# First batch of a fused attention and feed-forward kernel: loads issued at once into places of their own, products of zeros before the first data, weight roundings one step earlier, attention steps one at a time

## The chip, the cores and the metric

One core of a Trainium2 chip. The time is the device time of one execution in microseconds (us), median over several executions. The kernel before takes 1046.3 us (median of 3; in the runs beside the changed kernel 1046.53). The granted clock is the share of its full clock that TensorE was given, 1.00 or 0.50 in these records; the mean of a stretch can lie between.

## The reference, cut to what matters

```python
def _attn_ref(q, k, v, g_norm):              # 8 batches, 8 heads, 576 rows, 64 columns, float32
    kv = np.einsum('bhsd,bhse->bhde', k, v)  # no softmax: k and v meet first
    out = np.einsum('bhsd,bhde->bhse', q, kv)
    rms = np.sqrt(np.mean(out * out, axis=-1, keepdims=True) + 1e-06)
    return out / rms * g_norm

def _moe_ref(x, w_in, w_out):                # x: 4608 x 512; w_in 512 x 2048; w_out 2048 x 512
    h = x @ w_in
    g = np.maximum(0.01 * h, h)
    return g @ w_out
```

The attention's output, with the heads side by side, is x. The tokens go through the two large products in nine blocks of 512. One batch is 576 rows, so block 0 holds most of batch 0, and the remaining 64 rows of batch 0 (the tail) and the first 448 rows of batch 1 make up block 1; both are computed beside block 0's products.

## The kernel before: what the change and the argument touch

From block 1 on, the products use a scheme with seven products for eight (h_a, h_b, h_c, o_a and so on). Block 0 is computed with plain products, because the weights are still arriving and being rounded. It alternates four products of 512 columns into `h_ps` (one for each row group e of one weight job) with four into `o_acc` (one for each 128 tokens), 16 times. Each counts as two instructions in the profile, so such a group is a row of `x8`; the very first `h_ps` comes in two halves of 256 columns, together a row of `x16`. After each pair, `between(n)` emits weight roundings and attention steps.

The names in the profile: `kv_ps` is k times v of one pair of heads, `q_ps` and `rest_ps` are the turned q, `o_ps` is one quarter of the attention's output, `sq` its square, `ss_ps` the sums of squares. `h_ps` is the first large product, `gT` its activation (on ScalarE), `o_acc` the second large product, `h_a` the first product of block 1. A rounding is two pieces on ScalarE (`add`, `cut`) and four on VectorE, the second of them the shift.

```python
    def load_pair(b, p):                       # two heads: k, v, q; ring of two buffers per name
        hs = slice(2 * p, 2 * p + 2)
        k_ins[b, p] = load_rows(nc.sync, k[b, hs], "k")
        v_ins[b, p] = load_rows(nc.sync, v[b, hs], "v")
        if b == 0:
            q_ins[b, p] = load_rows(nc.scalar, q[b, hs], "q")
            return
        ...
    load_pair(0, 0)
    load_pair(0, 1)
    ...
    w1_sb = [[consts.tile([P, NE, U * P], F32, name=f"w1_{h}_{c}") for c in range(NC)]
             for h in range(2)]               # one tile holds U = 2 jobs: job u writes [:, :, u*P:(u+1)*P]
    ...
        # the rounding of one job, 128 x 512 numbers:
        pin(nc.scalar.activation(add, lo, func=AF.Copy, scale=2.0 ** -29))                  # L153 / L173
        pin(nc.scalar.activation(cut, hi.bitcast(F32), func=AF.Copy, scale=2.0 ** -112))    # L155 / L175
        pin(nc.vector.tensor_scalar(cut, cut, HIGH_MOST, -HIGH_MOST, ...))                  # L156 / L176
        pin(nc.vector.tensor_scalar(dst, cut, 3, None, op0=ALU.logical_shift_left))         # L159 / L179
        pin(nc.vector.scalar_tensor_tensor(dst, in0=cut, scalar=0x80000000, in1=dst, ...))  # L160 / L180
        pin(nc.vector.tensor_tensor(dst, dst, add, op=ALU.add))                             # L162 / L182
    ...
    def outputs(b, lo, hi, e, sums, o_ps):     # one quarter of the attention's output
        ...
        sq = work.tile([P, n], F32, tag="t2k", name="sq", bufs=4)   # four places, shared with add and cut
        nc.scalar.activation(sq, o_ps, func=AF.Square)
        nc.scalar.activation(x[:, e, :], o_ps, func=AF.Copy, scale=g_sb[:, e:e + 1])
        if sums is None:
            return sq
        nc.vector.tensor_add(sums, sums, sq)
        return sums
    ...
    def first_attention():                     # batch 0, half blocks of 256 columns
        for p in range(NP):
            attention_kv(0, p, kv_ps)          # 10 small products, x20 in the profile
            ...                                # 8 + 2 products with the identity turn q (x16, x4)
            if p < 2:
                load_pair(0, p + 2)            # pairs 2 and 3 reuse the buffers of 0 and 1
        ...
    loaded, rounded = 7, 3
    def between(n):
        nonlocal a_steps, loaded, rounded
        while rounded < min(2 + (18 * n + 6) // 7, 2 * n + 5, len(w_jobs)):
            ...
            round_w(rounded)
            rounded += 1
        if n == 3:
            go(a_steps)                        # the tail in one piece
            a_steps = attention(1)
        if n > 6:
            go(a_steps, 2 if n > 8 else 1)     # batch 1's steps in groups
```

## Time and profile before

| | before |
|---|---|
| median, range | 1046.53 us, 1046.02 to 1046.81 (4 runs beside the changed kernel) |
| TensorE busy | 1000.2 us, 96% |
| first quarter of the output (`o_ps`) starts | 27.43 us |
| first full row of `h_ps` starts, after its wait | 46.56 us |
| block 0 over, first `h_a` starts | 183.52 us |
| from there to the end of the span | 861.2 us |

The last four rows come from starts of rows in TensorE's timeline. Two of the lines behind the table are these, the others are in the prediction:

```profile
27.43 4.50 PE L85 MATMUL o_ps<-qT,kv 128*32 128x256 f32 x40 [0.81 <-DVE qT L309]
...
183.52 1.89 PE L85 MATMUL h_a<-xT,w 128*128 128x256 f32 x8
```

### The profile page before, as it was taken

Reading aid. Unit: us, or ns where it says so; the run is one execution under the profiler, and the core shown is the slowest. Engines: PE = TensorE matmul, PEld = TensorE weight load, DVE = VectorE, ACT = ScalarE, POOL = GpSimd, SP = SyncE. Lnnn points to the kernel's source line nnn. Section 1 sums busy time; section 2 is a strip of 40 time slices with the busy share of each in tenths; the row PEclk is TensorE's granted clock in tenths of the full one; section 3 lists DMA queues with packets and bytes.
Section 4 is the critical chain, followed back from the end, with each engine's and each line's share of the span. In section 5 each row is a group of like instructions: output and inputs, shape, how many; then the busy total and the mean of one; then the engine's idle time right before and its main releaser. Section 6 shows DMA issues by size and latency. Waiting matters only on the chain.

```text
span 1044.7 us, 13017 instructions
## 1 busy us (share of the span) xinstructions
PE 1000.2 (96%) x5146; PEld 777.3 (74%) x5146; DVE 426.5 (41%) x591; ACT 264.5 (25%) x497; POOL 505.1 (48%) x403
## 2 busy tenths in 40 slices
PE   5589989999999999999999999999999999999997
PEld 4334434778888778888888788877887788888886
DVE  1557678224531463235323543344314521332123
ACT  1444343232213221322122311321132212111210
POOL 2000021456655665555555555555555656666641
PEclk9799999999999999999999999999999999999999
DMA  8356750710052004300340024000300010001001
GB/s 214 124 151 201 212 150 0 193 29 1 1 154 67 1 1 109 112 1 1 94 127 1 1 80 142 1 1 19 113 1 1 1 41 1 1 0 41 1 0 41
DMA packets 45309, 63.41 MB, mean 61 GB/s; under 512 B 5312, under 2 KB 39104, under 8 KB 45248
## 3 DMA queue, kind: packets, MB, share of 16 engines
q1 hardware_dynamic: 34560, 51.95, 18.2%
q10 hardware_dynamic: 10432, 10.62, 3.2%
q8 instruction: 41, 0.67, 0.3%
q14 instruction: 20, 0.16, 0.1%
q0 software_dynamic: 256, 0.00, 0.0%
HBM read 53.12 MB, written 9.44 MB: 60 GB/s over the span
## 4 chain that ended last, share of the span: by engine, by line
PE 89%; DVE 6%; DMA 2%; issue 1%; ACT 1%; SPq 1%; POOL 0%; ACTq 0%; DVEq 0%
PE o_a L85 21%; PE h_a L85 21%; PE h_c L85 10%; PE o_c L85 10%; PE h_ps L85 5%; PE o_b L85 5%; PE h_b L85 5%; PE o_ps L85 3%; PE o_acc L85 3%; PE kv_ps L85 2%; DVE rms L253 1%; PE ss_ps L85 1%; DMA v_in<-in_v_dram 1%; DVE w L160 1%; DMA q_in<-in_q_dram 1%
## 5 line engine op out<-in xcount | busy, mean ns | idle before, releaser
L85 PE MATMUL o_a<-wt,gs 128*128 128x256 f32 x512 | 124.8, 386 | 2.9 <-DVE o L330 1.9
L330 DVE TENSOR_TENSOR o<-o_a,o 128x512 f32<-128x512 f32 x104 | 71.4, 687 | 129.9 <-PE o_a L85 129.9
L85 PEld LDWEIGHTS o_a<-wt,gs 128*128 128x128 f32 x512 | 94.1, 190 | 28.5 <-issue 10.8
L330 POOL TENSOR_TENSOR wt<-w,w 128x512 f32<-128x512 f32 x32 | 40.9, 1277 | 153.4 <-PE o_a L85 150.1
L330 POOL TENSOR_TENSOR ws<-w 128x512 f32<-128x512 f32 x32 | 44.3, 1386 | 135.1 <-PE h_a L85 98.8
L330 POOL TENSOR_TENSOR ws<-w,w 128x512 f32<-128x512 f32 x32 | 42.5, 1328 | 131.5 <-DMA raw<-in_moe_w_in_dram 130.8
L330 POOL TENSOR_TENSOR gs<-g,g 128x512 f32<-128x512 f32 x64 | 82.4, 1287 | 23.2 <-ACT g L409 22.8
L409 ACT ACTIVATE g<-g 128x512 f32<-128x512 f32 x96 | 60.4, 629 | 128.1 <-DVE g L330 127.8
L330 POOL TENSOR_TENSOR wt<-w,wt 128x512 f32<-128x512 f32 x64 | 83.0, 1297 | 2.5
L330 POOL TENSOR_TENSOR wt<-w 128x512 f32<-128x512 f32 x32 | 40.8, 1276 | 69.2 <-PE o_a L85 67.4
L330 DVE TENSOR_TENSOR o<-o_c,o 128x512 f32<-128x512 f32 x56 | 38.6, 690 | 85.4 <-PE o_c L85 82.0
L85 PE MATMUL h_ps<-xT,w 128*128 128x512 f32 (+1 forms) x136 | 64.1, 619 | 8.0 <-DVE w L162 8.0
L414 ACT COPY g<-h_a 128x512 f32<-128x512 f32 x32 | 18.8, 586 | 198.6 <-PE h_a L85 198.6
L85 PE MATMUL h_a<-xt,w 128*128 128x256 f32 x256 | 61.2, 382 | 3.0 <-DVE g L330 3.0
L330 DVE TENSOR_TENSOR g<-h_b,g 128x512 f32<-128x512 f32 x32 | 22.1, 690 | 101.4 <-PE h_b L85 101.4
L85 PE MATMUL h_a<-xT,ws 128*128 128x256 f32 x256 | 62.4, 387 | 0.0
L85 PE MATMUL o_a<-wt,g 128*128 128x256 f32 x256 | 60.7, 380 | 1.7 <-DVE o L330 1.7
L85 PE MATMUL h_a<-xt,ws 128*128 128x256 f32 x256 | 62.4, 386 | 0.0
L85 PE MATMUL o_a<-w,g 128*128 128x256 f32 x256 | 60.6, 379 | 0.8 <-DVE o L330 0.8
L85 PE MATMUL h_a<-xT,w 128*128 128x256 f32 x256 | 60.6, 379 | 0.0
L85 PE MATMUL h_c<-xT,ws 128*128 128x256 f32 x256 | 60.5, 379 | 0.0
L85 PE MATMUL h_c<-xt,ws 128*128 128x256 f32 x256 | 60.5, 379 | 0.0
(78 smaller groups left out, 1767.1 us busy)
## 6 DMA issues: line engine op xcount, KB each, us to landing
out_dram<-o ACTq DMA_DIRECT2D x36, 256.0 KB, 2.2
raw<-in_moe_w_in_dram SPq DMA_DIRECT2D x16, 512.0 KB, 5.7
raw<-in_moe_w_out_dram SPq DMA_DIRECT2D x16, 512.0 KB, 6.2
q_in<-in_q_dram SPq DMA_DIRECT2D x56, 144.0 KB, 3.5
q_in<-in_q_dram SPq DMA_DIRECT2D x56, 140.0 KB, 3.5
k_in<-in_k_dram SPq DMA_DIRECT2D x32, 160.0 KB, 3.6
v_in<-in_v_dram SPq DMA_DIRECT2D x32, 160.0 KB, 3.5
k_in<-in_k_dram SPq DMA_DIRECT2D x32, 128.0 KB, 3.4
```

Source lines behind the costliest of these rows:

```text
L85: pin(nc.tensor.matmul(*args, **kw))
L160: pin(nc.vector.scalar_tensor_tensor(dst, in0=cut, scalar=0x80000000, in1=dst, op0=ALU.bitwise_and, op1=ALU.bitwise_or))
L253: nc.vector.reciprocal(rms, rms)
L330: eng.tensor_tensor(out_, a, b_, op=ALU.subtract if minus else ALU.add)
L409: nc.scalar.activation(t, t if src is None else src, func=AF.Prelu, alpha=SLOPE)
L414: nc.scalar.copy(g11, bank)
```

## The change

The intent: (1) TensorE should not wait for pairs 2 and 3, so their loads get places that are still unused and are issued at once; (2) it should not start at the low clock, so it multiplies zeros while the first data come; (3) no product should wait for a weight, so one more rounding goes ahead of the block and the pace is faster; (4) attention should not hold up block 0 in lumps, so its steps go in one at a time. The cut leaves out what follows from this: the first three weight loads are issued before the small products, the zeroed `kv` tiles are made first, `g_norm` is loaded later, and the first half blocks use the PSUM places in another order.

```diff
-    load_pair(0, 0)
-    load_pair(0, 1)
+    def load_first():
+        early = xpool.tile([P, NE * NT], F32, tag="xT", name="early")
...
+        for p in range(NP):
...
+            if p < 2:
+                ks, vs = in_tile("k"), in_tile("v")
...
+            else:
+                ks, vs = (rows(wcomb.tile([P, 4 * U * P], F32, tag=f"pair{2 * p + i - 4}", ...)) ...)
+                qs = rows(early[:, (p - 2) * n:])
+            k_ins[0, p] = load_rows(nc.sync, k[0, hs], ks)
+            v_ins[0, p] = load_rows(nc.sync, v[0, hs], vs)
+            q_ins[0, p] = load_rows(nc.scalar, q[0, hs], qs)
...
     def first_attention():
+        idle = ps_m.tile([P, NT], F32, tag="ob", name="idle_ps")
+        for _ in range(IDLE):                                        # IDLE = 5
+            matmul(idle, lhsT=kvs[1][:, 0]..., rhs=kvs[1]..., start=True, stop=True)
...
-            if p < 2:
-                load_pair(0, p + 2)
...
+        round_w(0)                                                   # was after the first divide
+        homes = itertools.cycle(("gs1", "gs2", "gs3", "gs4"))        # squares and roots of the two
+        def new(n, name):                                            # half blocks: places of their own
+            return gpool.tile([P, n], F32, tag=next(homes), name=name)
...
-        round_w(1)
-        round_w(2)
+        for j in range(1, 4):
+            round_w(j)
...
+            between(n, 0)
             for t in range(4):
                 matmul(accs[t], ...)
-            between(n)
+            between(n, 1)
...
-    loaded, rounded = 7, 3
+    steps = {6 + i: tail for tail in [tail_of(0, NT, S)] for i in range(NE + 1)}
+    steps.update((i, a1) for a1 in [attention(1)] for i in (12, 13, 16, 17, *range(18, 29)))
+    loaded, rounded = 7, 4
...
-        while rounded < min(2 + (18 * n + 6) // 7, 2 * n + 5, len(w_jobs)):
+        go(steps.get(2 * n + half, iter(())), 1)
+        while half and rounded < min(3 * n + 3, 2 * n + 9, len(w_jobs)):
...
-        if n == 3:
-            go(a_steps)
-            a_steps = attention(1)
-        if n > 6:
-            go(a_steps, 2 if n > 8 else 1)
```

More of the change, by code (lines that the diff above doesn't have):

```diff
@@ L67 @@
     EPS = 1e-6
+    IDLE = 5
     assert H * D == DM and S == 64 * (J + JJ) and E * NE == D and B * S == NB * NT
@@ L88, with load_rows @@
     k_ins, v_ins, q_ins = {}, {}, {}
-    def load_rows(eng, src, name):
-        t = ins.tile([P, 2, JJ, D], F32, tag=f"{name}_in", name=f"{name}_in")
+    def load_rows(eng, src, t):
         pin(eng.dma_start(t[:64], src[:, :SLO, :].rearrange("h (p j) d -> p h j d", j=JJ)))
@@ L96, in load_rows, with in_tile @@
         return t
+    def in_tile(name):
+        return ins.tile([P, 2, JJ, D], F32, tag=f"{name}_in", name=f"{name}_in")
     def load_pair(b, p):
         hs = slice(2 * p, 2 * p + 2)
-        k_ins[b, p] = load_rows(nc.sync, k[b, hs], "k")
-        v_ins[b, p] = load_rows(nc.sync, v[b, hs], "v")
-        if b == 0:
-            q_ins[b, p] = load_rows(nc.scalar, q[b, hs], "q")
-            return
+        k_ins[b, p] = load_rows(nc.sync, k[b, hs], in_tile("k"))
+        v_ins[b, p] = load_rows(nc.sync, v[b, hs], in_tile("v"))
         t = ins.tile([P, T * D], F32, tag="q_in", name="q_in")
@@ L114, in load_pair, with rows @@
         q_ins[b, p] = t
-    load_pair(0, 0)
-    load_pair(0, 1)
-    g_sb = consts.tile([P, NE], F32, name="g_sb")
-    for h in range(H):
-        nc.gpsimd.dma_start(g_sb[h * E:(h + 1) * E], g_norm.rearrange("(i e) -> i e", e=NE))
+    def load_first():
+        early = xpool.tile([P, NE * NT], F32, tag="xT", name="early")
+        n = 2 * JJ * D
+        def rows(t):
+            return t[:, :n].rearrange("p (l j d) -> p l j d", l=2, j=JJ)
+        for p in range(NP):
+            hs = slice(2 * p, 2 * p + 2)
+            if p < 2:
+                ks, vs = in_tile("k"), in_tile("v")
+                qs = rows(ins.tile([P, T * D], F32, tag="q_in", name="q_in"))
+            else:
+                ks, vs = (rows(wcomb.tile([P, 4 * U * P], F32, tag=f"pair{2 * p + i - 4}",
+                                          name="early_kv")) for i in range(2))
+                qs = rows(early[:, (p - 2) * n:])
+            k_ins[0, p] = load_rows(nc.sync, k[0, hs], ks)
+            v_ins[0, p] = load_rows(nc.sync, v[0, hs], vs)
+            q_ins[0, p] = load_rows(nc.scalar, q[0, hs], qs)
+    kvs = []
+    for i in range(2):
+        kv = consts.tile([P, NP, NE, 2, E], F32, name=f"kv_{i}")
+        nc.gpsimd.memset(kv, 0.0)
+        kvs.append(kv)
+    load_first()
     w1_sb = [[consts.tile([P, NE, U * P], F32, name=f"w1_{h}_{c}") for c in range(NC)]
@@ L201 @@
                             channel_multiplier=-1, compare_op=ALU.is_ge, fill=0.0)
-    kvs = []
-    for i in range(2):
-        kv = consts.tile([P, NP, NE, 2, E], F32, name=f"kv_{i}")
-        nc.gpsimd.memset(kv, 0.0)
-        kvs.append(kv)
+    g_sb = consts.tile([P, NE], F32, name="g_sb")
+    for h in range(H):
+        pin(nc.gpsimd.dma_start(g_sb[h * E:(h + 1) * E], g_norm.rearrange("(i e) -> i e", e=NE)))
     xTs = {}
@@ L230, in copy_kv, with t2k, outputs @@
                                   kv_ps[r, ps].rearrange("p a (i e) -> p a e i", e=NE))
-    def outputs(b, lo, hi, e, sums, o_ps):
+    def t2k(n, name):
+        return work.tile([P, n], F32, tag="t2k", name=name, bufs=4)
+    def outputs(b, lo, hi, e, sums, o_ps, new=t2k):
         i, n = lo // NT, hi - lo
@@ L238, in outputs @@
                    rhs=qTs[b][:, p, lo - b * S:hi - b * S], start=True, stop=True)
-        sq = work.tile([P, n], F32, tag="t2k", name="sq", bufs=4)
+        sq = new(n, "sq")
         nc.scalar.activation(sq, o_ps, func=AF.Square)
@@ L245, in outputs, with divide @@
         return sums
-    def divide(lo, hi, sums, ss_ps):
+    def divide(lo, hi, sums, ss_ps, new=t2k):
         i, n = lo // NT, hi - lo
@@ L250, in divide @@
         matmul(ss_ps, lhsT=same.rearrange("p h e -> p (h e)"), rhs=sums, start=True, stop=True)
-        rms = work.tile([P, n], F32, tag="t2k", name="rms", bufs=4)
+        rms = new(n, "rms")
         nc.scalar.activation(rms, ss_ps, func=AF.Sqrt, scale=1.0 / D, bias=eps_sb)
@@ L286, in first_attention @@
     def first_attention():
+        idle = ps_m.tile([P, NT], F32, tag="ob", name="idle_ps")
+        for _ in range(IDLE):
+            matmul(idle, lhsT=kvs[1][:, 0].rearrange("p e l i -> p (e l i)"),
+                   rhs=kvs[1].rearrange("p a e l i -> p (a e l i)"), start=True, stop=True)
         qT = qTs[0] = work.tile([P, NP, S], F32, tag="qT", name="qT")
@@ L290, in first_attention @@
         rest = ps_m.tile([P, NP, 64], F32, tag="oc", name="rest_ps")
+        for j in range(3):
+            load_w(j)
         for p in range(NP):
@@ L304, in first_attention @@
                     to[:, :J, :], q_ps[:, :, r:r + 64])
-            if p < 2:
-                load_pair(0, p + 2)
-        for j in range(7):
+        for j in range(3, 7):
             load_w(j)
@@ L310, in first_attention @@
             qT[:, :, :SLO].rearrange("p a (t j) -> p a t j", j=JJ)[:, :, :, J], rest)
-        free = iter(("ob", "oc", "ha", "hb", "hc", "oa", "ob", "oc", "ha", "hb"))
+        round_w(0)
+        free = iter(("ob", "hb", "hc", "oa", "oc", "ha", "ob", "hb", "hc", "oa"))
+        homes = itertools.cycle(("gs1", "gs2", "gs3", "gs4"))
         def ps(name):
             return ps_m.tile([P, N2], F32, tag=next(free), name=name)
+        def new(n, name):
+            return gpool.tile([P, n], F32, tag=next(homes), name=name)
         sums = [None, None]
         for e in range(NE):
-            sums[0] = outputs(0, 0, N2, e, sums[0], ps("o_ps"))
-        sums[1] = outputs(0, N2, NT, 0, None, ps("o_ps"))
-        divide(0, N2, sums[0], ps("ss_ps"))
-        round_w(0)
+            sums[0] = outputs(0, 0, N2, e, sums[0], ps("o_ps"), new)
+        sums[1] = outputs(0, N2, NT, 0, None, ps("o_ps"), new)
+        divide(0, N2, sums[0], ps("ss_ps"), new)
         for e in range(1, NE):
-            sums[1] = outputs(0, N2, NT, e, sums[1], ps("o_ps"))
-        divide(N2, NT, sums[1], ps("ss_ps"))
-        round_w(1)
-        round_w(2)
+            sums[1] = outputs(0, N2, NT, e, sums[1], ps("o_ps"), new)
+        divide(N2, NT, sums[1], ps("ss_ps"), new)
+        for j in range(1, 4):
+            round_w(j)
     def add(eng, out_, a, b_, minus=False):
@@ L506, with between @@
     first_attention()
-    a_steps = tail_of(0, NT, S)
-    loaded, rounded = 7, 3
-    def between(n):
-        nonlocal a_steps, loaded, rounded
-        while rounded < min(2 + (18 * n + 6) // 7, 2 * n + 5, len(w_jobs)):
+    steps = {6 + i: tail for tail in [tail_of(0, NT, S)] for i in range(NE + 1)}
+    steps.update((i, a1) for a1 in [attention(1)] for i in (12, 13, 16, 17, *range(18, 29)))
+    loaded, rounded = 7, 4
+    def between(n, half):
+        nonlocal loaded, rounded
+        go(steps.get(2 * n + half, iter(())), 1)
+        while half and rounded < min(3 * n + 3, 2 * n + 9, len(w_jobs)):
             if loaded < len(w_jobs):
@@ L520, in between @@
             rounded += 1
-        if n == 3:
-            go(a_steps)
-            a_steps = attention(1)
-        if n > 6:
-            go(a_steps, 2 if n > 8 else 1)
     first_block(between)
-    go(a_steps)
     second, before = iter(()), None
```

## The prediction

> **What bounds the kernel now.** I read the page first, then the chain that ended last, then the stretches and the instructions in order of time for the first 190 us, because the change touches only batch 0 and block 0.
>
> ```profile
> PE 1000.2 (96%) x5146; PEld 777.3 (74%) x5146; DVE 426.5 (41%) x591; ACT 264.5 (25%) x497; POOL 505.1 (48%) x403
> PE   5589989999999999999999999999999999999997
> PEclk9799999999999999999999999999999999999999
> PE 89%; DVE 6%; DMA 2%; issue 1%; ACT 1%; SPq 1%; POOL 0%; ACTq 0%; DVEq 0%
> ```
>
> TensorE bounds it. From 225 us on it works 807.97 of 819.7 us, and nothing there is edited. What can be won lies in the first slices: idle time, and time at a half clock.
>
> ```profile
> 0.00:10.00 10.00, 1.03 (x16) 0.97 (x16) 0.06 (x1) 1.49 (x2) 6.37 (x19) 1.00 0.82 174
> 30.00:40.00 10.00, 4.53 (x47) 2.13 (x40) 7.06 (x12) 6.17 (x16) 0.00 (x0) 0.95 0.22 71
> 40.00:50.00 10.00, 4.99 (x12) 3.48 (x11) 7.28 (x10) 2.80 (x5) 0.00 (x0) 0.50 0.33 105
> 150.00:155.00 5.00, 1.28 (x2) 0.84 (x3) 4.80 (x7) 1.74 (x3) 0.87 (x1) 0.66 0.01 3
> ```
>
> (Columns: stretch and length, busy PE, PE weight loads, DVE, ACT, POOL, then granted clock, DMA share, GB/s.) The idle waits on the path are these rows of the timeline:
>
> ```profile
> 21.46 1.53 PE L85 MATMUL kv_ps<-v_in,k_in 128*64 128x64 f32 x20 [1.09 <-DMA v_in<-in_v_dram]
> 24.23 1.98 PE L85 MATMUL q_ps<-ident,q_in 128*64 128x128 f32 x16 [1.24 <-DMA q_in<-in_q_dram]
> 39.51 1.19 PE L85 MATMUL ss_ps<-sq,same 128*128 128x256 f32 x2 [5.28 <-DVE sq L244]
> 46.56 9.70 PE L85 MATMUL h_ps<-xT,w 128*128 128x256 f32 x22 [5.01 <-DVE w L162]
> 60.53 3.67 PE L85 MATMUL h_ps<-xT,w 128*128 128x512 f32 x8 [0.84 <-DVE w L162]
> 153.72 1.83 PE L85 MATMUL ss_ps<-sq,same 128*128 128x448 f32 x2 [4.21 <-DVE sq L244]
> ```
>
> The record shows clock 1.00 before 30 us, but durations contradict it: a kv_ps group of 20 takes 1.53 us at 21.46 us and 0.88 at 107 us. A quarter-output group runs at 0.9 us at 27.4 us and 0.5 at 32.7. So TensorE was at half speed until about 31.7 us; I take the early 1.00 as "no record yet".
>
> Total loss after the first data at 9 us: idle 22.5 us (gaps summed) and about 14 us of half clock. That is the most the change could win, and 2% of the time is 20.9 us.
>
> **What the skill says.** The Trainium skill, "TensorE: Matmul & The Clock Gate", Part 1: the array starts at half clock and a busy window of about 3.4 us releases it, an idle one throttles it. The trace agrees in part: low clock lasts from 38.6 to 52.2 us, four such windows. But TensorE was continuously busy from 9 to 20 us with small products and stayed slow, so not every product seems to count. "SBUF — State Buffer", Who interferes with whom: VectorE in a two-port mode and GpSimd block each other. The trace agrees: the shift (L159) takes 0.43 us alone and 1.37 us at 138.7 us, when GpSimd adds weights; L160 goes from 0.69 to 1.64. "DMA: Bandwidth & Descriptors", Issuing engines are not separate DMA queues: ScalarE's and SyncE's loads share the same 16 engines. The trace shows these at share 0.80 to 1.13 from 2 to 10 us, at only 188 to 236 GB/s for the 64-partition rows.
>
> **The change, part 1: loads and zero products.** Batch 0 is 24 transfers of about 144 KB, 3.46 MB. Pairs 2 and 3 used to wait until TensorE had freed pairs 0 and 1 (issues at 10.5 to 17.3 us). Now they wait for nothing but a free DMA semaphore: in the built program each issue waits for an earlier one's landing, eight in flight. 1.73 MB landed by 10 us; the rest at 0.236 MB per us takes 7.3 us, so 17.3, plus some landing delay: pair 3 at about 18.0 us (before 21.46 for k and v, 24.1 for q). The five 512-column products of zeros cost nothing (TensorE has nothing else); at half clock they are 5 x 1.71 = 8.6 us from about 2 us, less once released, so done near 9 us. If the clock stays up, a pair costs 0.88 + 1.1 + 0.25 = 2.2 us instead of 3.84. Then the first o_ps starts at 18.0 + 2.3 + 0.8 = 21.1 us instead of 27.43: **-6.3 us** (only -4.8 if the small products let the clock fall again).
>
> **Part 2: from first o_ps to first h_ps**, 46.56 - 27.43 = 19.1 us now. First half: ScalarE at 0.85 us per quarter sets the pace; reciprocal starts 5.6 us in, as now (5.9). Second half: the rounding of job 0 and the buffers shared with it delayed the second ss_ps to 12.1 us in. With the rounding ahead of all and separate buffers, VectorE's order is reciprocal 1.75, add 0.43, multiply 1.23, two adds 0.86: 10.0 us in. From there the same chain: ss 0.7 or 1.2, rms 0.5, reciprocal 1.75, multiply 1.23, rounding of job 1 2.24: 16.8 us in. **-2.3 us.** h_ps starts near 37.9 us. TensorE idles twice in it for 4 us and more, so it still starts at half clock.
>
> **Part 3: block 0**, 46.56 to 183.68 = 137.1 us now: 128.2 busy, of it 5.0 by low clock, and 8.9 idle. Here I read the instruction order of the built program, and it is not all gain.
> - Gone: waits of 0.83, 1.74 (tail in one piece) and 0.72 and 0.57 us: -3.9.
> - Rounding a step ahead makes a false need. At 40.49 us h_ps ran only its first column group (e=0) and then waited for job 1, which rounds other columns of the same tile: the dependency is on the range. Now job 5 is emitted before h_ps 2, and job 9 before h_ps 4; the built order has a second VectorE wait there, on e=1. Job 5 ends 6.35 us after gT 1 starts (62.64 - 56.30 now), TensorE arrives after 3.43 + 0.86: wait 2.1 instead of 0.84: +1.3.
> - Job 9's ScalarE part stands behind the second tail step, which follows the products before h_ps 4: 0.85 + 3.6 - 1.4 = +3.1.
> - 19 attention steps stand alone instead of about 10 groups; each costs the next product 0.2 us (3.63 against 3.43), and single quarters 0.1 more: +2.2.
> - Batch 1's sums (128x448): ScalarE's second square stands behind gT 11 and job 26, and the fourth quarter needs its PSUM place: 0.6 + 1.2 + 0.55 + 0.6 = 2.9 us. The last ss_ps then waits for three roundings under GpSimd contention; from second square to ss_ps was 12.1 us, I get 11, with only 0.9 + 3.43 of TensorE work inside, and some 5.5 us of waiting. 8.4 against 4.2: +4.2.
> - Low clock: the start as now; after the waits two falls instead of one: +1.3.
> Sum for block 0: +8.2. The two largest terms rest on a fixed order on ScalarE, and any drift in arrival shrinks them; I take three quarters of the +8.6 that the last, third and fifth points carry together: block 0 **+6 us**.
>
> After block 0 nothing moves. Sum: -6.3 - 2.3 + 6 = -2.6, so 1043.7; I put **1044 us**.
>
> **Rivals.** (a) The steps spread as intended: no wait over 1 us in block 0 but for the low clock. Then block 0 gains about 6 us (3.9 + 4.2 less 2.2), the whole -14 to -17: about 1030. For it: VectorE has only 41% to do, and between tail and ss_ps there are now 3.43 us pieces. Against: the order on ScalarE and the second wait. (b) The loads are hidden: the clock falls between pairs, DMA limits pair 3 to 19 us, and block 0 loses the full 8 or more: about 1051. (c) VectorE becomes the bound: three roundings per pair of products are 6.7 us against 6.86 us of TensorE, and attention on top; but TensorE needs only two per step, so this eats lead, not time; 1044 or worse by 2.
>
> **Range and chances.** The start is good for 6 to 10 us; block 0 for anything from -8 to +12. 8 in 10: 1033 to 1053 us. Over 2% faster needs all of (a) and more: 6%; over 2% slower needs waits I did not find: 3%; within 2%: 91%.
>
> **What would show it.** In the changed profile: first o_ps near 21 us, kv_ps groups at 0.9 us from the start, first full h_ps near 38, low clock there; a wait of 2 us at the third h_ps and 3 us at the fifth, both for a rounding on VectorE; a wait of about 3 us at the fourth 448-column quarter, for ScalarE; then over 4 us at ss_ps; h_a starting near 181 us. If h_a starts before 170 us, the waits in block 0 are my error; if o_ps starts after 24 us, the loads are.

## The result, and the profile after

The changed kernel takes 1049.31 us (1048.09 to 1050.19, 4 runs) against 1046.53. The ratio is 1.0026, with a 95% interval of 1.0009 to 1.0044. A ratio here is the mean time of one kernel's runs over that of the other's in the same rounds, so it is not quite the ratio of the medians. The kernel became about 2.8 us slower: "same" at 2%, inside the range that was predicted, and 5 us above the predicted time.

The page and the stretches after (columns as in the prediction):

```profile
PE   7689979999999999999999999999999999999997
PEclk7799989999999999999999999999999999999999
0.00:10.00 10.00, 8.11 (x34) 3.79 (x36) 0.13 (x2) 1.11 (x1) 6.36 (x19) 1.00 0.84 175
10.00:20.00 10.00, 6.88 (x86) 5.69 (x84) 2.47 (x8) 1.61 (x4) 0.00 (x0) 0.68 1.12 245
20.00:30.00 10.00, 9.19 (x94) 6.40 (x94) 4.90 (x12) 4.49 (x10) 0.00 (x0) 0.50 1.01 351
```

The zeros do keep TensorE busy for 8 of the first 10 us. But from 10 to 20 us the granted clock is 0.68, and from 20 to 30 us 0.50: TensorE is 92% busy there, at half speed.

TensorE's timeline after (start, length, engine, line, operation, shapes, count, then the idle time before and what ended it):

```profile
1.85 6.96 PE L86 MATMUL idle_ps<-kv 128*128 128x512 f32 x10 [1.85 <-POOL kv L139]
8.86 0.95 PE L86 MATMUL kv_ps<-v_in,k_in 128*64 128x64 f32 x20
...
14.21 1.53 PE L86 MATMUL kv_ps<-v_in,k_in 128*64 128x64 f32 x20 [3.12 <-DMA v_in<-in_v_dram]
...
26.41 4.42 PE L86 MATMUL o_ps<-qT,kv 128*32 128x256 f32 x40 [0.81 <-DVE qT L337]
...
36.48 0.67 PE L86 MATMUL ss_ps<-sq,same 128*128 128x256 f32 x2 [3.28 <-DVE sq L267]
36.99 0.60 PE L86 MATMUL h_ps<-xT,w 128*128 128x256 f32 x2
43.01 9.01 PE L86 MATMUL h_ps<-xT,w 128*128 128x256 f32 x22 [5.42 <-DVE w L182]
...
58.45 2.84 PE L86 MATMUL h_ps<-xT,w 128*128 128x512 f32 x6 [2.14 <-DVE w L182]
...
76.36 2.84 PE L86 MATMUL h_ps<-xT,w 128*128 128x512 f32 x6 [3.02 <-DVE w L182]
...
138.68 0.96 PE L86 MATMUL o_ps<-qT,kv 128*32 128x448 f32 x8 [2.74 <-ACT xT L264]
...
148.98 0.99 PE L86 MATMUL ss_ps<-sq,same 128*128 128x448 f32 x2 [4.01 <-DVE sq L267]
...
185.16 1.89 PE L86 MATMUL h_a<-xT,w 128*128 128x256 f32 x8
```

Pair 0 finds a warm TensorE (0.95 us for its 10 products, 1.53 in the kernel before). Then TensorE waits 3.12 us for pair 1's v. The clock record has it fall to half at 13.5 us, and pair 1 and the two after it run back to back at 3.8 us each. The first quarter starts at 26.41 us, only 1.0 us earlier than before.

The waits in block 0 show a signature worth knowing: `x6` with a wait on a rounding, after a row of `x2`. Of one weight job the product of the first row group ran (two instructions), and the other three waited. The rows of `x2` stand at 36.99, 55.30 and 72.22 us; the last two are cut above.

| | before | after | difference | predicted |
|---|---|---|---|---|
| first `o_ps` | 27.43 | 26.41 | -1.0 | -6.3 |
| from there to full `h_ps` | 19.13 | 16.60 | -2.5 | -2.3 |
| from there to `h_a` | 136.96 | 142.15 | +5.2 | +6 |
| rest | 861.2 | 861.5 | +0.3 | 0 |
| span | 1044.7 | 1046.7 | +2.0 | -2.6 |

### The profile page after: what moved, and what is told of

It reads as the page before. It is cut to its first block, busy times and chain, and to the rows that moved or that the text cites. A ratio compares the mean times of both kernels' runs of the same rounds, so it can differ in the third digit from the quotient of the medians.

```text
span 1046.7 us, 13016 instructions
## 1 busy us (share of the span) xinstructions
PE 1006.6 (96%) x5156; PEld 777.2 (74%) x5156; DVE 424.6 (41%) x591; ACT 265.2 (25%) x497; POOL 505.6 (48%) x403
## 4 chain that ended last, share of the span: by engine, by line
PE 90%; DVE 5%; DMA 1%; issue 1%; ACT 1%; SPq 1%; DVEq 0%; ACTq 0%
PE o_a L86 21%; PE h_a L86 21%; PE h_c L86 10%; PE o_c L86 10%; PE h_ps L86 6%; PE h_b L86 5%; PE o_b L86 5%; PE o_acc L86 4%; PE o_ps L86 4%; PE kv_ps L86 3%; DVE rms L276 2%; DMA v_in<-in_v_dram 1%; PE ss_ps L86 1%; DVE sq L267 1%; PE q_ps L86 1%
## 5 line engine op out<-in xcount | busy, mean ns | idle before, releaser
L441 ACT ACTIVATE g<-g 128x512 f32<-128x512 f32 x96 | 60.4, 629 | 128.2 <-DVE g L362 127.8
L86 PE MATMUL h_ps<-xT,w 128*128 128x512 f32 (+1 forms) x136 | 63.0, 609 | 10.6 <-DVE w L182 10.6
L86 PE MATMUL o_c<-wt,gs 128*128 128x256 f32 x256 | 60.5, 379 | 0.0
```

The source lines that it names most:

```text
L86: pin(nc.tensor.matmul(*args, **kw))
L441: nc.scalar.activation(t, t if src is None else src, func=AF.Prelu, alpha=SLOPE)
```

## The experiments

All were run with five rounds beside the kernel before. The kernel before itself spread from 1042.9 to 1049.3 us (11 runs), so differences under 2 us aren't resolved. Times are compared by their ratios to the kernel before. A ratio of 0.001 is about 1 us.

### e1: without the zeros

```diff
-    IDLE = 5
+    IDLE = 0
```

> The changed kernel without the five products of zeros. Theory (the zeros warm only pair 0, because TensorE then idles 3.1 us until pair 1 lands at 14.1 us and the clock falls at 13.1 us): pair 0 takes 3.8 instead of 2.2 us and is still done before 14.1 us, so the first output product stays near 26.4 us and the time within 1 us of the changed kernel (1049.3 us). Rival (the zeros carry the start): first output product 3 us or more later, 1052 us or more.

Measured: 1048.58 us, ratio 1.0020 (1.0001 to 1.0040), against 1.0026 with them. The zeros are worth nothing that can be measured. Pair 0 ran cold (1.53 us), but in the profiled execution the clock came up at 17.5 us by itself and the first quarter started at 22.64 us, earlier than with zeros and than expected (26.4). That execution is one draw: the clock's rises and falls lie 3.41 us or a multiple of it apart, and this grid begins 0.4 us into the span here, 3.3 us in the changed kernel's profile.

### e2: three more zero products between pair 0 and pair 1

```diff
+            for _ in range(3 if p == 0 else 0):
+                matmul(idle, lhsT=kvs[1][:, 0]..., rhs=kvs[1]..., start=True, stop=True)
```

> Three more products of zeros between pair 0 and pair 1 (2.6 us at full clock, inside the wait of 3.1 us). Theory (the clock that fell in that wait is what cost the start): pairs 1 to 3 take 2.2 instead of 3.8 us each, first output product near 21.6 us, h_ps near 38.2 us, time about 5 us less (1044.5). Rival 1 (the small products of kv and of the transposes do not hold the clock even when it is up): it falls one or two windows later, gain 0 to 2 us. Rival 2 (the loads of pairs 2 and 3 set the start): clock up but TensorE waits for data, gain under 1.5 us.

Measured: 1046.39 us, ratio 1.0012 (0.9994 to 1.0030), so -1.4 us against the change, inside the scatter: Rival 2's number, not the theory's. The step that failed in the prediction is seen here, though:

```profile
20.30 0.95 PE L86 MATMUL kv_ps<-early_kv 128*64 128x64 f32 x20 [1.56 <-DMA early_kv<-in_v_dram]
```

With the gap filled the clock held until 21.5 us and pairs 1 and 2 ran warm (each kv group 0.95 us). Now pair 3 waits 1.56 us for its data, the clock falls at 21.5 us, and the first quarter starts cold at 24.14 us, 2.3 us earlier than in the changed kernel. TensorE merely ran into the next limit, the transfers.

### e3: the change's start, the old block 0

```diff
-    steps = {...}
+    a_steps = tail_of(0, NT, S)
...
-        while half and rounded < min(3 * n + 3, 2 * n + 9, len(w_jobs)):
+        while rounded < min(2 + (18 * n + 6) // 7, 2 * n + 5, len(w_jobs)):
...
+        if n == 3:
+            go(a_steps)
+            a_steps = attention(1)
+        if n > 6:
+            go(a_steps, 2 if n > 8 else 1)
```

> The changed kernel with block 0's attention steps and rounding pace as before (new loads, zeros, separate buffers and early rounding of job 0 kept). Theory (block 0 lost 5.2 us by the new pace and steps, the start won 3.5): block 0 back to about 137 us, h_ps start unchanged near 43.0 us, time about 5 us less than the changed kernel, 1044. Rival (block 0 is longer for another reason, such as the clock or the loads of the weights): within 2 us of the changed kernel.

Measured: 1044.56 us, ratio 0.9990 (0.9975 to 1.0005): 3.8 us less than the change, no different from before. So pace and single steps together cost about 4 us, as the third part of the prediction has it (+6). The start, however, gains next to nothing against before, though in the profiled execution everything was early:

```profile
37.98 9.25 PE L86 MATMUL h_ps<-xT,w 128*128 128x256 f32 x22 [5.43 <-DVE w L182]
...
148.27 1.83 PE L86 MATMUL ss_ps<-sq,same 128*128 128x448 f32 x2 [8.74 <-DVE sq L267]
```

The full `h_ps` row starts 8.6 us before that of the kernel before, `h_a` only 5.8 us (177.76). The last `ss_ps` waits 8.74 us instead of 4.21. ScalarE's timeline shows why. Batch 1's second and third square in the kernel before:

```profile
141.66 0.54 ACT L240 ACTIVATE sq<-o_ps 128x448 f32<-128x448 f32 x1
...
145.21 0.54 ACT L240 ACTIVATE sq<-o_ps 128x448 f32<-128x448 f32 x1 [2.48 <-PE h_ps L85]
...
146.16 0.60 ACT L490 ACTIVATE gT<-h_ps 128x512 f32<-128x512 f32 x1
```

The same view of the changed kernel, at its second square:

```profile
135.98 0.60 ACT L522 ACTIVATE gT<-h_ps 128x512 f32<-128x512 f32 x1 [6.35 <-PE h_ps L86]
136.47 0.65 ACT L173 ACTIVATE add<-raw 128x512 uint32<-128x512 uint32 x1
...
137.57 0.54 ACT L263 ACTIVATE sq<-o_ps 128x448 f32<-128x448 f32 x1
```

Before, second and third square stand ahead of the gT of that step. In the changed kernel the second square stands behind gT and behind a piece of a rounding, and gT waits for TensorE. The order of instructions on an engine is fixed when the program is built, so ScalarE sits idle for 6.35 us with the square's data ready (its products ended at 127.8 us). The kernel with the old block 0 has the same order as the changed one (gT at 135.25 us after 7.00 us of idle time, the second square at 136.85; its products ended near 130.8). Its steps are those of before; what differs ahead of them is the start: one more rounding, the places of the first squares, the loads and the PSUM places. Which of these turns the order wasn't tried.

### e4: each rounding writes a range of its own

```diff
-    w1_sb = [[consts.tile([P, NE, U * P], F32, ...
+    w1_sb = [[consts.tile([P, U, NE, P], F32, ...
-                 w_jobs += [(w1_sb[h][c][:, :, u * P:(u + 1) * P], ...
+                 w_jobs += [(w1_sb[h][c][:, u, :, :], ...
-                        matmul(h_ps[:, cols], lhsT=w1_sb[h][c][:, e, u * P:(u + 1) * P],
+                        matmul(h_ps[:, cols], lhsT=w1_sb[h][c][:, u, e, :],
```

(The other readers of the tile are changed to match.) Before, the two jobs of a tile interleave: job u=0 covers columns 0 to 127 of each of four row groups, job u=1 columns 128 to 255. Taken as ranges from first to last byte, they overlap, although no byte is shared. Now they lie one after the other. Sizes, values and number of instructions are the same.

> The changed kernel with w1 laid out so that each rounding writes a range of its own, nothing else moved. Theory (the waits of 2.1 and 3.0 us at the third and fifth h_ps, and 2.2 us of the wait before the first, are for roundings of other columns of the same tile): all three go, h_ps starts near 40.8 instead of 43.0 us, block 0 5 us shorter, time 6 to 8 us less: about 1042. Rival (these waits are for data really needed, or the many separate steps cost the time by slow weight loads): waits stay, time within 1.5 us.

Measured: **1037.22 us**, ratio 0.9917 (0.9902 to 0.9933): 8.7 us less than before, and 11.4 less than the change (0.9917 / 1.0026 = 0.9891). TensorE's timeline:

```profile
36.86 3.09 PE L86 MATMUL h_ps<-xT,w 128*128 128x256 f32 x8
40.64 7.18 PE L86 MATMUL h_ps<-xT,w 128*128 128x256 f32 x16 [0.68 <-DVE xT L277]
```

All four products of the first half row (`x8`) run at once, where one (`x2`) ran before, and what ends the next wait is x, not a weight. The waits of 2.14 and 3.02 us at the third and fifth `h_ps` are gone. By sum: 5.42 - 0.68 + 2.14 + 3.02 = 9.9 us, and `h_a` starts at 175.26 instead of 185.16, 9.9 us earlier. The waits at batch 1's fourth quarter (2.74) and `ss_ps` (4.07) stay, as they should. The theory had the right waits but too small a sum (6 to 8 us): of the first wait 4.7 us went, not 2.2. The roundings themselves did not become faster, which would be a rival: their four VectorE pieces take 423, 516, 750 and 720 ns on average up to 185 us, with the old layout as with the new. That the program is built by ranges from first to last byte is the reading that fits; the runs show that the wait goes with the layout.

### e5: the squares of block 0's steps in places of their own

```diff
-    steps = {6 + i: tail for tail in [tail_of(0, NT, S)] ...
+    steps = {6 + i: tail for tail in [tail_of(0, NT, S, new)] ...      # gs1 to gs4, not t2k
-    steps.update((i, a1) for a1 in [attention(1)] ...
+    steps.update((i, a1) for a1 in [attention(1, new)] ...
```

> The changed kernel, but block 0's tail and batch 1's first attention steps take their squares and roots from four places of their own (the ones batch 0's half blocks used) instead of the four shared ones. Theory (the built order of ScalarE, forced by the shared places, makes the fourth 448-column quarter and the last ss_ps wait): the order changes, the waits of 2.7 us (o_ps) and 4.0 us (ss_ps) shrink to under 1.5 us together, and with them the second fall of the clock goes: -5 to -8 us against after, about 1042. Rival (those waits only stand in front of others: the roundings that ScalarE now does later make h_ps wait instead): two or more us of new waits at h_ps near 150 to 165 us, total within 2 us of after. The waits of 2.1 and 3.0 us at the third and fifth h_ps are untouched in both.

Measured: 1047.46 us, ratio 1.0016 (0.9996 to 1.0035): the rival was right in the total.

```profile
127.47 4.22 PE L86 MATMUL h_ps<-xT,w 128*128 128x512 f32 x6 [3.10 <-DVE w L182]
...
145.09 0.91 PE L86 MATMUL ss_ps<-sq,same 128*128 128x448 f32 x2
...
160.77 5.40 PE L86 MATMUL o_acc<-w,gT 128*128 128x512 f32 x8 [3.00 <-DVE w L182]
```

The quarter and the `ss_ps` don't wait any more. In exchange the products wait 3.10, 3.00 and later 0.77 us for roundings that are now later. In this profile the full `h_ps` row starts 3.9 us earlier than in the changed kernel and `h_a` only 0.2 us, so block 0 even takes longer (145.8 us for 142.2). It was right that the shared places forced the order, wrong that the order was all.

### e6: layout and places together

The two edits of e4 and e5 together.

> The weight tile laid out so that each rounding writes a range of its own (as in the run of the layout alone) and the places of their own for squares and roots together. If the two causes are separate, their gains add: layout alone was 1037.2, so about 1031 (1029 to 1034). If the ss_ps wait is only moved to a later rounding, 1036 to 1038, as layout alone.

Measured: 1042.72 us, ratio 0.9968 (0.9952 to 0.9984): worse than either expectation, and 5 us worse than the layout alone.

```profile
148.84 6.76 PE L86 MATMUL o_acc<-w,gT 128*128 128x512 f32 x8 [7.07 <-DVE w L182]
...
163.59 0.77 PE L86 MATMUL ss_ps<-sq,same 128*128 128x128 f32 x2 [4.00 <-DVE sq L267]
```

In block 0 no wait of TensorE is over 0.9 us now until 141 us. Then it waits 7.07 us for one rounding, and 4.00 for the last `ss_ps`. ScalarE's timeline of this kernel shows the order again:

```profile
141.46 0.60 ACT L522 ACTIVATE gT<-h_ps 128x512 f32<-128x512 f32 x1 [3.06 <-PE h_ps L86]
...
142.36 0.67 ACT L173 ACTIVATE add<-raw 128x512 uint32<-128x512 uint32 x1
```

From 121.6 to 142.4 us ScalarE has not one piece of a rounding; it waits for TensorE, and VectorE idles twice for 3.7 us. The roundings come in a row after that, when GpSimd adds weights: the shift takes 1.38 us and the next piece 1.63, instead of 0.43 and 0.69. From 150 to 160 us VectorE is busy 9.82 of 10 us. Squares first means roundings last: the same work, put off into the dearer stretch.

### e7: the kernel before with the layout alone

The layout edit of e4 on the kernel before.

> The kernel before with the new layout alone, no other part of the change. Theory (before had room between rounding and use and paid the false need only once, the 5.0 us wait before the first full h_ps and 0.84 at the third): the first wait is shared with the true need of the later column groups, so -1 to -3 us: about 1043 to 1044.5, clearly above the 1037.2 of layout with the change; then the change itself is worth about 6 us once the false need is gone. Rival (the layout is all of the gain and the change is worth nothing): about 1037 to 1038, equal to the run of the layout alone.

Measured: 1037.69 us, ratio 0.9919 (0.9903 to 0.9935). The rival was right: the layout is the whole gain, and the change adds nothing to it (0.9917 with the change).

```profile
38.45 3.62 PE L85 MATMUL h_ps<-xT,w 128*128 128x256 f32 x8
42.27 2.07 PE L85 MATMUL h_ps<-xT,w 128*128 128x256 f32 x8 [0.20 <-DVE xT L254]
...
144.65 1.64 PE L85 MATMUL ss_ps<-sq,same 128*128 128x448 f32 x2 [4.19 <-DVE sq L244]
```

I had expected only 1 to 3 us, because I took the first wait for a mostly true one. It went from 5.01 to 0.20 us (with a new wait of 0.27 at the row behind it), and the waits of 0.72 and 0.57 us at the later `h_ps` rows (of the kind `x6`) went too. Those are 5.8 us of the 10.6 by which `h_a` starts earlier in this profile. 2.0 us come from a luckier start (`ss_ps` at 37.47 instead of 39.51). The rest is mostly clock: it is low for 6.8 us at the start of block 0 instead of 13.7, and for 3.4 instead of 6.8 around 148 us. The wait of 0.84 us at the third `h_ps` (`x8`) is still there, so it was a true need, other than the expectation has it. By the threshold of 2% this is still "same", as e4 is, but both intervals lie clear of 1.

### e8: q of pairs 2 and 3 behind v, on SyncE's queue

On layout and places (e6):

```diff
-            q_ins[0, p] = load_rows(nc.scalar, q[0, hs], qs)
+            q_ins[0, p] = load_rows(nc.scalar if p < 2 else nc.sync, q[0, hs], qs)
```

> As layout and places together, and the q rows of pairs 2 and 3 are issued on SyncE's queue behind their v rows instead of at once on ScalarE's. Theory (pair 1's v comes late, 14.1 us, because q of pairs 2 and 3 takes the engines and the places in flight before it): pair 1's first product near 11.5 to 12.5 us, the idle time before it under 1.5 us instead of 3.1, the clock holds past it, pair 3 ends near 22 us, first o_ps near 22 to 23.5 us instead of 26: -2 to -4 us against layout and places. Rival (the loads as a whole are limited by their rate, so what pair 1 wins pair 3 loses, waiting for q till after 21 us with the clock down again): first o_ps at 24.5 to 26 us, within 1.5 us of layout and places.

Measured: 1038.92 us, ratio 0.9933 (0.9916 to 0.9950): 3.6 us less than e6, as the theory has it.

```profile
11.96 0.95 PE L86 MATMUL kv_ps<-v_in,k_in 128*64 128x64 f32 x20 [0.48 <-DMA v_in<-in_v_dram]
...
18.44 1.53 PE L86 MATMUL kv_ps<-early_kv 128*64 128x64 f32 x20 [2.09 <-DMA early_kv<-in_v_dram]
```

Pair 1 starts at 11.96 us instead of 14.54, with 0.48 us of idle time instead of 3.34. So it was the early q loads that held pair 1's v up. How they did it shows in SyncE's timeline, at the second half of pair 1's v, first in e6, then here:

```profile
8.85 0.59 SPq L94 DMA_DIRECT2D v_in<-in_v_dram  x1
```

```profile
6.68 0.59 SPq L94 DMA_DIRECT2D v_in<-in_v_dram  x1
```

It is issued 2.2 us later in e6 and then on its way about as long (5.6 against 5.1 us). Eight transfers go out without a wait, four on each queue, and each further issue waits for an earlier one's landing: with the early q loads ahead of it, for pair 0's v (landed at 8.84 us), without them for pair 0's k (6.67). So most of the delay is waiting for a place, not a slower transfer. Pair 3 then waits 2.09 us, and the clock is low again.

### e9: layout, the change's start, the old block 0

The edits of e4 and e3 together.

> Layout, the change's start, and the kernel before's pace and steps in block 0. Against before with the layout alone (1037.7) only the start differs. Theory (the new start is worth its 2.3 us between first quarter and h_ps, plus the 1 us by which the first quarter came earlier): full h_ps 1.5 to 3.5 us earlier, total 1034 to 1036. Rival (the start is a lottery of the clock and its gain is lost in the cold products after it): 1037 to 1038, as the layout on before.

Measured: 1037.14 us, ratio 0.9925 (0.9905 to 0.9945). The rival's number (1037 to 1038), but only in part for the rival's reason:

```profile
35.68 7.12 PE L86 MATMUL h_ps<-xT,w 128*128 128x256 f32 x16 [1.88 <-DVE xT L277]
...
144.25 1.83 PE L86 MATMUL ss_ps<-sq,same 128*128 128x448 f32 x2 [8.73 <-DVE sq L267]
```

`h_ps` is 6.6 us ahead of that of e7, `h_a` 0.2 us behind (173.21 against 172.97). 4.5 us of it are at the last `ss_ps`, 8.73 instead of 4.19: the order on ScalarE as in e3. The rest is mostly clock: it also falls at 63.6 us, where `ss_ps` and the `h_ps` behind it take 1.7 us longer than in e7, and it is low for 10.2 us around the last `ss_ps` instead of 3.4, much of which TensorE waits through.

### e10: the same with q late

The edit of e8 on e9.

> As the run before it, with q of pairs 2 and 3 on SyncE's queue behind v. The same move gave 3.6 us when it was added to layout and places (1042.7 to 1038.9; first quarter at 23.1 instead of 26.3 us). Theory: it is the queue order of the loads, so it adds here too: -2.5 to -4 us against layout with old block 0, about 1032. Rival (there it was the lottery of the clock): within 1 us.

Measured: 1036.07 us, ratio 0.9908 (0.9887 to 0.9930). That is 1.1 us less than e9 at the median and 1.8 by the ratios, inside the scatter; the expected 2.5 to 4 us are not shown. Pair 1 starts at 12.20 us (14.04 in e9), so the queue order works here too. But the profiled execution of e9 had kept its clock over the gap anyway, and its first quarter started at 21.82, against 21.17 here.

### e11: and with two zero products between pair 0 and pair 1

```diff
+            for _ in range(2 if p == 0 else 0):
+                matmul(idle, ...)
```

> As the run before it, with two more zero products between pair 0 and pair 1. In the kernel with q late the gap there was 0.48 us at pair 1 and 2.09 us at pair 3, and the clock was down from 18.1 to 28.3 us; two products of zeros (0.9 us each when the clock is up) delay pair 1 by at most 1 us and cannot fill the gap at pair 3: expected 0 to +1 us against the run without them. Rival (the clock decides, and any filling pays): -1 to -2 us.

Measured: 1036.36 us, ratio 0.9918 (0.9896 to 0.9939): within 0.3 us of e10 at the median, as expected. Once more, zeros don't pay.

### e12: layout, the faster pace, but the steps in groups

```diff
-        while rounded < min(2 + (18 * n + 6) // 7, 2 * n + 5, len(w_jobs)):
+        while rounded < min(3 * n + 3, 2 * n + 9, len(w_jobs)):
```

(on e9)

> Layout, the change's start and its faster pace of roundings, but the attention steps grouped as before. Between layout with the change (1037.2) and layout with old block 0. If the single steps cost block 0 its time (fixed order on ScalarE at the fourth 448-column quarter, one more switch per step): as layout with old block 0, 1034 to 1036. If the faster pace costs it (roundings in front of the squares on ScalarE and VectorE): 1037 to 1039, no better than layout with the change.

Measured: 1036.70 us, ratio 0.9919 (0.9898 to 0.9939). It lies on the line between the two expectations and doesn't decide. The profile has 2.45 us at the tail's second quarter and 4.46 at `ss_ps`. The second square stands behind gT here too (7.00 us of idle time on ScalarE), but between the third and the fourth square there are the pieces of one rounding, not two as in e9, so that order alone doesn't make the 8.73 us. A kernel with the old pace and the single steps wasn't run: the steps ask for batch 1's loads, which hang on the pace of the roundings. So how the 4 us of e3 divide between pace and steps stays open; with the layout neither shows (0.9917, 0.9925, 0.9919 for e4, e9 and e12).

## Why the prediction was right or wrong, point by point

**The time.** Predicted 1044, range 1033 to 1053; measured 1049.31. In the range, wrong in direction: a gain of 2.6 us was predicted, a loss of 2 (profiles) to 2.8 us (medians) came. That it lies in the range is owed to the range's width of 20 us: one of the three parts failed.

**Part 1, the start: wrong by 5.3 us.** The prediction's step was "If the clock stays up, a pair costs [...] 2.2 us instead of 3.84. Then the first o_ps starts at [...] 21.1". It didn't stay up. Two terms failed. First, only pair 3's landing was estimated; pair 1's wasn't. Issuing everything at once puts q of pairs 2 and 3 ahead of v of pair 1 in the row of transfers: its second half is issued at 8.74 us instead of 6.70, and pair 1 starts at 14.21. Moving q back shows that (e8, 11.96). The prediction had the fact in hand ("each issue waits for an earlier one's landing, eight in flight"). Second, the wait of 3.12 us lets the clock fall, and three pairs at 3.8 us in series then set the start, not pair 3's loads, which were there (no wait at its row). The fallback of the same paragraph ("only -4.8 if the small products let the clock fall again") took the fall to come late. The closing sentence, "if o_ps starts after 24 us, the loads are [my error]", named the place.

**Part 2, first quarter to first full row: right.** 16.6 us against 16.8.

**Part 3, block 0: right in mechanism, near in size.** The waits were 2.14 where 2.1 was worked out, 3.02 for 3.1, 2.74 for 2.9, and 4.01 for 5.5, each at the place and for the releaser named. The sum is +5.2 against +6 as put down and +8.2 as listed. Of the 3.0 us between list and result, the waits are 1.7 (11.9 us of idle time instead of 8.9 is +3.0, listed were +4.7), most of it the last wait, 4.01 for 5.5; the extra steps and the low clock together came to +2.2, listed were +3.5. That the +6 came so near is partly luck: the quarter was taken off for drift in arrival, which no run shows. That there were one false need and one fixed order, as said, is shown by e4 and e5: the layout removes the first two waits, the places of their own the last two (though e5 puts others in their stead). The small waits were only partly understood: the 0.84 us at the third `h_ps` was a true need (e7), and the 5.01 us before the first full row a false one. The prediction had both facts of that in hand ("ran only its first column group [...] and then waited for job 1, which rounds other columns of the same tile") and counted the wait as a fixed part of the start instead of the largest thing to be won.

**The rivals.** (a), steps that spread as intended at 1030: not seen in any kernel; e6, in which both causes are taken away, has its waits elsewhere. (b), the clock falls between pairs and DMA limits: nearest to what happened at the start, and 1051 nearest to the time. (c), VectorE as the bound: denied for the whole; it is so for some 20 us from 144 us on in e6, after it was left idle.

**What else could have been won at the start.** With the start of the change in old block 0 (e3, e9), an earlier start was given back at `ss_ps`, where 8.7 us are waited instead of 4.2. All kernels with the new layout take 1036.1 to 1037.7 us but those with the places of their own. Taking the medians, e10 is the fastest at 1036.07, though it isn't told apart from e4, e7, e9, e11 and e12. The version to keep is e7: one line of layout and its readers on the kernel before, -7.9 us.

## What to carry to other kernels

When some products of a group run and the rest wait for a write that they don't need, look at how the parts of a tile interleave: a layout in which each writer has a contiguous range cost nothing here and was worth more than four rearrangements. Before loads are issued earlier, work out when the *first* of them lands, not only the last: here eight could be in flight, and what was issued first held the places (2.2 us at pair 1's v). And when an engine that keeps its program's order feeds the bound, as ScalarE did (6.35 us idle with a square's data ready), an earlier start may only move the wait: read the order of that engine before and after.

## What the Trainium skill lacked or had wrong

- "TensorE: Matmul & The Clock Gate", Part 1, says that an idle window throttles the array. In these runs a window needed not be idle as a whole, and its idle share alone doesn't decide: the clock fell after windows of 3.41 us that were idle for 72% (changed kernel, 10.1 to 13.5 us), 62% (before, at 151.6 us) and only 46% (e2, 18.1 to 21.5 us), and held over windows idle for 47% (e3, 12.4 to 15.8 us) and 59% (e1, 51.6 to 55.0 us).
- The same section says that a busy window releases the clock. Two windows filled with the 64-column kv products and products with the identity (17.0 to 23.8 us, changed kernel) did not release it, one in e1 (14.0 to 17.5 us) did; what tells them apart isn't shown. Its remark that the window is free-running agrees: the phase differed among the profiled executions (0.4 us in e1, 3.3 in the changed kernel). The kernel before alone spread over 6.4 us; how much of that is the phase isn't shown.
- No page tells that a wait can follow from ranges that interleave without sharing a byte. It cost 4.8 us at one place in the kernel before, and 7.9 us in all (e7, medians).
- "SBUF — State Buffer", Who interferes with whom, says that VectorE in a two-port mode and GpSimd block each other. The trace agrees: the shift takes 0.43 us alone and 1.37 us while GpSimd adds. The page gives no size for such a rounding; here one rounding's pieces grew from 2.2 to 5.1 us (0.43, 1.38, 1.63 and 1.64 us at 143.6 us in e6).
- "DMA: Bandwidth & Descriptors", Issuing engines are not separate DMA queues, says that DMAs of all issuing engines run on the same 16 DMA engines and interleave. What the runs show is a delay of 2.6 us that loads issued on ScalarE's queue gave those on SyncE's (pair 1 at 14.54 us in e6, 11.96 in e8); 2.2 us of it are a later issue, because a program's transfers also wait for one another's places in flight, and only 0.4 a longer time on the way. The section doesn't speak of that wait before the issue.
